# A fused attention and feed-forward kernel: a rebuilt opening, and pair sums of pattern tiles moved from VectorE to DMA transfers

## The chip, the cores and the metric

The kernel runs on one core of a Trainium2 chip. The core has five engines that run side by side, each through its own list of instructions in order: TensorE (PE in the profile) for matrix products, ScalarE (ACT) for functions such as the exponential, VectorE (DVE) for elementwise work, GpSimd (POOL), and SyncE (SP), which issues DMA transfers. They meet only through semaphores. The metric is the device time of one execution in microseconds (us); the median of several runs is given.

## The reference

The kernel computes a transformer layer in its parallel form: one normalised input feeds an attention with 32 query heads and one shared key and value head, and a feed-forward part with a squared ReLU. Both results are added to the input.

```python
S, D, H, Dh, F = 2048, 640, 32, 20, 1536
xn = layernorm(x)                                    # over the last axis, no scale or shift
q = (xn @ wq).reshape(1, S, H, Dh).transpose(0, 2, 1, 3)
k, v = xn @ wk, xn @ wv                              # one head of keys and values for all queries
p = softmax(einsum("bhqd,bkd->bhqk", q, k) * Dh ** -0.5)
o = einsum("bhqk,bkd->bhqd", p, v)
a = o.transpose(0, 2, 1, 3).reshape(1, S, H * Dh) @ wo
h = relu(xn @ w1 + b1) ** 2
out = x + a + h @ w2 + b2
```

## The kernel before, in words

**Blocks and tiles.** The queries are cut into 4 stretches of 512, the heads into 8 groups of 4. A stretch and a group make a block, and there are 32 blocks, worked off one after the other. Within a block the 2048 keys are 16 key tiles of 128. The scores of one key tile, one head and 512 queries are one tile of 128 x 512 in one of the eight banks of PSUM, so there are 32 x 16 x 4 = 2048 score tiles. Two to four of them are made at a time by matmuls that occupy different rows of TensorE's array (a score group). Everything else on TensorE runs as column groups: four matmuls side by side on 32 columns each.

**Two ways to an exponential.** ScalarE takes two or three neighbouring banks per instruction and writes the exponentials into slots of `PT` (`make_act`, L972; the instruction is L976). TensorE then multiplies them with the values (`make_pv`). The other way is a *set*: the four tiles of one key tile. VectorE makes from each tile of scores a line in the exponent of a bf16 number (`after_dqk`, instruction L1161, written as integers); three more copies, shifted by whole steps of the exponent's fraction, are made by GpSimd (L1181, an addition of 64-bit integers) or by VectorE (L1183). The weighted sum of the four copies stands for the exponential. So TensorE reads four pattern tiles for a set, two with the values `vx` and two with scaled values `vxs` (`make_dpv`). Where VectorE adds two of the copies beforehand (L1195, 128 x 2048 in one instruction, `dst = dst + src`), TensorE reads one column group less. A set that GpSimd and VectorE work on is kept in buffers of `tmore` and, once the input is no longer needed, of `x_sb`.

**The order.** The instruction lists are not written by hand. A planner in the kernel's own Python builds them: it keeps for each engine a queue of candidates with an assumed duration and assumed handover times (`Op`, `commit`, `LATS`), takes at each step the candidate that could start first, and orders ties by priorities (`prio`). `RULES` sets such priorities anew for each stage of 10 us of ScalarE's planned time, and `DEFAULTS` holds what no rule sets. Landings of DMA transfers are assumed too (`lat`), with a margin `DMARG` of 4 us. The plan decides the order on each engine and the semaphores that are waited for; on the chip each engine then goes through its list as fast as the waits let it. So the plan also decides how many tiles go to ScalarE and how many to sets.

**The opening.** The input's 16 row tiles (`x_sb`) are loaded, their mean and variance come from VectorE (L469 to L472) or, for the rows in `ACTST`, from ScalarE (L464, L465). Rows 0 to 3 get their reciprocal root by Newton steps on VectorE (L489 to L493), the others by a power on GpSimd (L481). L483 normalises a row, on VectorE or, for the rows in `POOLXN`, on GpSimd. TensorE transposes it with an identity matrix (L530 for rows 0 to 3, L594 for the others); the result is copied to `xnT`, by ScalarE (L532) or VectorE (L597). Keys follow (L546 for rows 0 to 3 one by one, `unit_KT` and L608 for four rows at a time), then queries and values. The identity is made by writing a staircase of zeros and one column of ones to DRAM (L428) and reading it back with a shifted stride (L435). Matmuls on constants (L525, L565) keep TensorE busy before.

**The other work.** The feed-forward part (L702, L710) and the output projections are cut into units that the planner puts between the score groups. A finished block is normalised by a chain of small transfers on SP's queue (`emit_norm`): sums to DRAM, back as a column (into `R`), their reciprocal on VectorE (L1048), to DRAM again, spread over the rows, and a product on VectorE (L1070). Eight transfers issued by GpSimd add the input to a tensor in DRAM on their way (L806).

The functions that the change touches:

Of the kernel before, what the change touches and what calls it, by code (L numbers as in the profile page):

```python
# [7 lines left out]
BF16 = mybir.dt.bfloat16  # L8
F32 = mybir.dt.float32
# [29 lines left out]
def _pl(z):  # L39
# [8 lines left out]
PTR = 20  # L48
# [3 lines left out]
STATIC = False  # L52
# [8 lines left out]
ADS = 1  # L61
# [5 lines left out]
NT = 9  # L67
# [7 lines left out]
DMEND = 1.0  # L75
SWITCH = 0.105
WARM = 0.72
WARM0 = 0.9

HOLD = dict(wq="TE2", b1="TE5", w1=("TE4", "TE6", "TE8", "TE10"), w2=("RL3_2", "RL3_4", "RL3_6", "RL3_8"), wo=("RL3_10", "FE24"), b2="VE8",  # L80
# [9 lines left out]
         2: {'KEEP': 1, 'JIT': 0.9},  # L90
         3: {'M1': 1},
         4: {'M1': 0, 'DRATE': 0.7, 'R3': 0, 'M1T': 0, 'PBIAS': 5},
         5: {'PVA': 1, 'SQP': 3, 'KEEP': 2},
         6: {},
         7: {'QKP': 0, 'D1P': 1, 'KEEP': 3},
         8: {'MPRIO': 0.9, 'ADP': 5, 'R3': -1},
         9: {'ADDN': 0.4, 'ND': 2},
         10: {'ADDN': 0.2, 'SQP': 0.7, 'M1T': 0, 'DRATE': 0.8, 'D1P': 1, 'URG': 3, 'JIT': 1.1, 'R3': 2},
         11: {'ADDB': 1, 'URG': 4, 'PP': 4, 'DRATE': 0.7, 'PVD': 0.9},
         12: {'ADDB': 1, 'BEHIND': 0.12, 'ADP': 0.9, 'DLAST': 2},  # L100
         13: {'EPS': 0},
         14: {'NOPEN': 1, 'EPS': 0.06, 'R3': 9, 'PP': 4},
         15: {'NOPEN': 1, 'EPS': 0.06, 'R3': 9, 'PP': 4, 'MRG': 0, 'DGAP': 0.8, 'ADP': 0.9},
         16: {'URG': 3, 'EVP': 0.3},
         17: {'ADDN': 0.2, 'M1T': 1.2},
         18: {'ADDN': 0.2, 'M1T': 1.2, 'MPRIO': 1.05},
         19: {'ADDN': 0.2, 'M1': 2, 'IDLE': 0.3, 'ND': 3, 'D1P': 0.5, 'ADP': 0.35, 'PVA': 1.05, 'QKP': 0},
         20: {'ADDN': 0.2, 'M1': 2, 'IDLE': 0.3, 'ND': 3, 'KEEP': 2, 'URG': 4, 'PP': 4, 'SQP': 3, 'ADP': 0.9},
         21: {'ADDN': 0.2, 'M1': 2, 'IDLE': 0.3, 'ND': 3, 'KEEP': 2, 'URG': 4, 'PP': 4, 'SQP': 3, 'ADP': 0.9, 'EPS': 0.12},
         22: {'PP': 2.5, 'NOPEN': 4},  # L110
         23: {'MPRIO': 0.3},
         24: {'PVD': 2.1, 'MPRIO': 1.05},
         25: {'DLAST': 2, 'EPS': 0, 'ADP': 0.35, 'ND': 3, 'R3': 1},
         26: {'NOPEN': 2, 'EVP': 0.3, 'EPS': 0.12},
         27: {'MRG': 0, 'URG': 2},
         28: {'ND': 1, 'ADP': 2, 'IDLE': 0.3},
         29: {'PBIAS': 0.6, 'M1': 2, 'ADDN': 0, 'SQP': 2},
         30: {},
         31: {'MRG': 0},
         32: {'NOPEN': 4, 'M1T': 0.6},  # L120
         33: {'NOPEN': 4, 'M1T': 0.6, 'MRG': 0, 'ADP': 3.5},
         34: {'R3': -1},
         35: {'ADDN': 0, 'DQP': 0.5, 'EPS': 0.12, 'MPRIO': 0.3},
         36: {'ADDN': 0, 'DQP': 0.5, 'EPS': 0.12, 'MPRIO': 0.3, 'NOPEN': 1},
         37: {'EVP': 1.1, 'ND': 2, 'M1T': 0.6},
         38: {'EVP': 1.1, 'ND': 2, 'M1T': 0.6, 'PBIAS': -1, 'PP': 0.9, 'PVA': 0.9},
         39: {'D1P': 1, 'ADP': 2},
         40: {'D1P': 1, 'ADP': 2, 'NOPEN': 2},
         41: {'D1P': 1, 'ADP': 2, 'NOPEN': 2, 'QKP': 0, 'JIT': 0.9},
         42: {'URG': 2, 'NOPEN': 2},  # L130
         43: {'URG': 2, 'NOPEN': 2, 'D1P': 1, 'DRATE': 0.7},
         44: {'PP': 2.5, 'R3': 1, 'NOPEN': 1, 'ADDN': 0},
         45: {'IDLE': 0.3, 'URG': 4, 'EVP': 0.8},
         46: {'IDLE': 0.3, 'URG': 4, 'EVP': 0.8, 'SQP': 3, 'ADDN': 0.6},
         47: {'IDLE': 0.3, 'URG': 4, 'EVP': 0.8, 'SQP': 3, 'ADDN': 0.6, 'DRATE': 0.8, 'DQP': 3},
         48: {'QKP': 0, 'M1T': 0.9, 'ADDN': 0.2, 'R3': 1},
         49: {'KEEP': 0, 'MPRIO': 0.5, 'DRATE': 0.7, 'R3': 0, 'NOPEN': 2},
         50: {'MRG': 0, 'URG': 2},
         51: {'MRG': 0, 'URG': 2, 'PVD': 1, 'DLAST': 6, 'M1T': 0},
         52: {'D1P': 3, 'R3': -1, 'DQP': 3},  # L140
         53: {'D1P': 1, 'KEEP': 1, 'PVD': 1, 'ADDN': 0, 'NOPEN': 1, 'DGAP': 1.5},
         54: {'D1P': 1, 'KEEP': 1, 'PVD': 1, 'ADDN': 0.2, 'NOPEN': 1, 'DGAP': 1.5, 'PBIAS': 5},
         55: {'D1P': 1, 'KEEP': 1, 'PVD': 1, 'ADDN': 0.2, 'NOPEN': 1, 'DGAP': 1.5, 'PBIAS': 1.5},
         56: {'D1P': 1, 'KEEP': 1, 'PVD': 1, 'ADDN': 0.2, 'NOPEN': 1, 'DGAP': 1.5, 'PBIAS': 1.5, 'URG': 3, 'ADP': 2},
         57: {},
         58: {'PVD': 0.9, 'DLAST': 3.5},
         59: {'ADDN': 0, 'EVP': 1.1, 'MRG': 0, 'DLAST': 3.5},
         60: {'ADDN': 0, 'EVP': 1.1, 'MRG': 0, 'DLAST': 3.5, 'M1T': 0, 'DGAP': 0},
         61: {},
         62: {'DGAP': 0.5, 'ADDN': 0.2, 'M1T': 0, 'JIT': 0.6, 'MRG': 9},  # L150
         63: {'DGAP': 0.5, 'ADDN': 0.2, 'M1T': 0, 'KEEP': 1, 'EVP': 0.8, 'IDLE': 0.3},
         64: {'PP': 0.9, 'NOPEN': 1, 'JIT': 0.9},
         65: {'DQP': 3, 'ADDN': 0, 'ADP': 2, 'NOPEN': 2},
         66: {'DQP': 3, 'ADDN': 0, 'ADP': 2, 'NOPEN': 2, 'ADDB': 1},
         67: {'ND': 1, 'R3': 1, 'PVA': 1, 'ADP': 2, 'D1P': 0.5},
         68: {'R3': -1, 'URG': 4}}
HOOK = None
PRIO = {}
NBEF = {}
# [14 lines left out]
QCPOS = 0  # L174
ACTST = (2, 5, 6)
POOLXN = (7, 9, 10, 11, 13, 14, 15)
# [8 lines left out]
DEFAULTS = dict(EVP=EVP, PBIAS=PBIAS, MPRIO=MPRIO, DGAP=DGAP, DLAST=DLAST, DRATE=DRATE, BEHIND=BEHIND, IDLE=IDLE, URG=URG, NOPEN=NOPEN,  # L185
                EPS=0.03, MRG=MRG, M1=M1, M1T=M1T, ADDN=ADDN, ADDB=0, ADP=3.5, JIT=JIT, R3=R3, STATIC=STATIC, PVA=1.05, PVD=1.05, D1P=0.5, PP=2.5, SQP=2, DQP=3, QKP=0, ND=2, WARM=WARM, KEEP=KEEP)

# [36 lines left out]
class Op:  # L224
    def __init__(self, name, eng, dur, parts, deps=(), lat=None, lock=False, mode="C", prio=3, dma=None):
        self.name, self.eng, self.dur, self.parts = name, eng, dur, parts
        self.deps = [d for d in deps if d is not None]
        self.lat, self.lock, self.mode, self.prio = lat, lock, mode, prio
        self.dma = dma
        self.start = self.fin = None  # L230
        self.consumed = False
        self.tgt = None
        self.clock = None
        self.frees = None
        self.after = None
        self.nb = 0.0
        self.blk = None
        if dma is not None:
            dma.n += 16
            self.tgt = (dma, dma.n)  # L240

    def ready(self):
        t = self.nb
        for d in self.deps:
            if d.fin is None:
                return None
            t = max(t, d.fin + (d.lat if d.lat is not None else LATS.get((d.eng, self.eng), 0.1)))
# [3 lines left out]
def bass_parallel_sum__grouped_kv_mqa__dense_activation_squared_relu__prompt_kernel(nc, A_x, A_wq, A_wk, A_wv, A_wo, B_x, B_w1, B_b1, B_w2, B_b2, out):  # L251
    es = ExitStack()
    with es:  # L253
# [59 lines left out]
        idd = nc.dram_tensor("idd", [128 * 128], BF16, kind="Internal").ap()  # L313
# [6 lines left out]
        eng_ctr = {k: newctr("m_" + k.lower()) for k in ENG if k != "SP"}  # L320
        osem = [newctr(f"osem{i}") for i in range(NOS)]
# [11 lines left out]
        lock_free = [0.0]  # L333
        pe_mode = ["C"]
# [9 lines left out]
        def commit(op):  # L344
# [4 lines left out]
            op.start, op.fin = s, s + op.dur  # L349
            free[op.eng] = op.fin  # L350
# [47 lines left out]
        def load(name, eng, fn, land, deps=()):  # L398
            return op(name, eng, 0.5, fn, deps, lat=land - 0.5, dma=one())
# [10 lines left out]
        stair = PT[:, PTR - 1, 0:128]  # L410
        z_ = op("idz", "DVE", 0.1, lambda e: e.memset(stair, 0.0), prio=-6)
        o_ = op("ido", "DVE", 0.08, lambda e: e.memset(stair[:, 0:1], 1.0), [z_], prio=-5)
# [6 lines left out]
        idw = []  # L419
# [8 lines left out]
        idw.append(load("IW", "SP", lambda e: e.dma_start(idd[0:128 * 128].rearrange("(p n) -> p n", p=128), stair), 2.2, [o_]))  # L428
# [5 lines left out]
        idd_rows = bass.AP(idd.tensor, 0, [[127, 128], [1, 128]])  # L434
        c_id = load("IR", "SP", lambda e: e.dma_start(ident[:], idd_rows), 2.2, idw)  # L435
        l_wq = load("wq", "SP", lambda e: e.dma_start(wq_sb[:, :, 80:D], wqv[:, :, 80:D]), 8.0, [HOLD["wq"]])
        w1v = B_w1.rearrange("(p dt) f -> p dt f", p=128)
        l_w1 = [load(f"w1{k}", "SP", lambda e, k=k: e.dma_start(w1_sb[:, :, 384 * k:384 * k + 384], w1v[:, :, 384 * k:384 * k + 384]), 8.0, [HOLD["w1"][k]]) for k in range(4)]
        l_b1 = load("b1", "SP", lambda e: e.dma_start(b1row[:], B_b1.rearrange("(f p) -> f p", p=128)), 8.0, [HOLD["b1"]])
        w2v = B_w2.rearrange("(ft p) d -> p ft d", p=128)  # L440
        l_w2 = [load(f"w2{k}", "SP", lambda e, k=k: e.dma_start(w2_sb[:, 3 * k:3 * k + 3, :], w2v[:, 3 * k:3 * k + 3, :]), 8.0, [HOLD["w2"][k]]) for k in range(4)]
        wov = A_wo.rearrange("(c p) n -> p c n", p=128)
        l_wo = [load(f"wo{c0}", "SP", lambda e, c0=c0, c1=c1: e.dma_start(wo_c[:, c0:c1, :], wov[:, c0:c1, :]), 8.0, [HOLD["wo"][k]]) for k, (c0, c1) in enumerate(((0, 3), (3, NCH)))]
# [14 lines left out]
        def rows(st):  # L458

            p = ROWP[st // 4]  # L460
# [1122 lines left out]
```

## Time and profile before

| | |
|---|---|
| median of 3 runs | 702.53 us (702.27 to 707.2) |
| profiled execution, from the first to the last instruction | 695.6 us |
| median less that span | 6.9 us |
| TensorE busy | 678.3 us, 98% |
| ScalarE busy | 673.4 us, 97% |
| VectorE busy | 606.7 us, 87% |
| GpSimd busy | 471.5 us, 68% |
| mean granted TensorE clock | 0.993, and 0.77 in the first 22 us |
| first and last exponential of ScalarE | starts at 22.05 us, ends at 686.7 us |

The profiled execution is one execution; its span leaves out what lies before the first and after the last instruction, and its own device time is taken as span and 6.9 us, which is the median. Matmuls are pipelined and the profile models their ends, so TensorE's 98% is the share of time with some matmul under way and not a share of its peak. The rows of the profile give for a group of instructions the line of the kernel, the engine, the operation, what is written and read, the shapes and the count; behind the bar the time in which at least one of them ran, the mean duration of one in nanoseconds, and the engine's idle time just before them with what ended it.

### The profile page before, as it was taken

Reading aid. Unit: us, or ns where it says so; the run is one execution under the profiler, and the core shown is the slowest. Engines: PE = TensorE matmul, PEld = TensorE weight load, DVE = VectorE, ACT = ScalarE, POOL = GpSimd, SP = SyncE. Lnnn points to the kernel's source line nnn. Section 1 sums busy time; section 2 is a strip of 40 time slices with the busy share of each in tenths; the row PEclk is TensorE's granted clock in tenths of the full one; section 3 lists DMA queues with packets and bytes.
Section 4 is the critical chain, followed back from the end, with each engine's and each line's share of the span. In section 5 each row is a group of like instructions: output and inputs, shape, how many; then the busy total and the mean of one; then the engine's idle time right before and its main releaser. Section 6 shows DMA issues by size and latency. Waiting matters only on the chain.

```text
span 695.6 us, 22438 instructions
## 1 busy us (share of the span) xinstructions
PE 678.3 (98%) x9683; PEld 214.6 (31%) x9685; DVE 606.7 (87%) x1028; ACT 673.4 (97%) x731; POOL 471.5 (68%) x474
## 2 busy tenths in 40 slices
PE   5899999999999999999999999999999999999997
PEld 3432223233222233332322233332322233333223
DVE  5859899998899998899789988889899998998984
ACT  4899999999999999999999999999999999999994
POOL 0526758788768877667558575787746756786873
PEclk7999999999999999999999999999999999999999
DMA  5414722257342221210200111011200211111101
GB/s 170 125 41 125 181 79 79 89 139 177 85 99 47 51 67 42 57 50 23 53 24 16 34 32 56 23 51 33 55 24 21 99 38 41 50 39 32 32 12 40
DMA packets 42304, 44.07 MB, mean 63 GB/s; under 512 B 15828, under 2 KB 33060, under 8 KB 42076
## 3 DMA queue, kind: packets, MB, share of 16 engines
q1 hardware_dynamic: 39420, 37.00, 19.2%
q0 software_dynamic: 2208, 5.25, 3.8%
q8 instruction: 76, 1.25, 0.7%
q10 hardware_dynamic: 576, 0.38, 0.2%
q14 instruction: 24, 0.20, 0.1%
HBM read 28.06 MB, written 14.94 MB: 62 GB/s over the span
## 4 chain that ended last, share of the span: by engine, by line
ACT 92%; PE 5%; DMA 1%; SPq 0%; DVE 0%; issue 0%; DVEq 0%
ACT PT L976 92%; PE ps L402 4%; DMA ident<-idd 1%; PE ps L594 1%; PE ps L530 0%; SPq L422 0%; DVE out_sb L1256 0%; PE ps L622 0%; PE ps L565 0%; PE ps L551 0%; SPq L430 0%; DVE PT L1256 0%; DVEq L253 0%; SPq L428 0%; DVE hT_tmp L408 0%
## 5 line engine op out<-in xcount | busy, mean ns | idle before, releaser
L976 ACT ACTIVATE PT<-ps 128x1024 bf16<-128x1024 f32 (+1 forms) x709 | 663.3, 1216 | 2.4 <-PE ps L402 2.4
L1161 DVE TENSOR_SCALAR tmore<-ps 128x512 uint16<-128x512 f32 x600 | 390.9, 685 | 49.0 <-PE ps L402 43.2
L1181 POOL INT64_ADD x_sb<-tmore x245 | 252.2, 1045 | 70.8 <-DVE tmore L1195 21.7
L1181 POOL INT64_ADD tmore<-tmore x196 | 201.3, 1041 | 115.7 <-DVE big L710 39.9
L402 PE MATMUL ps<-qT,kT 20*128 20x512 bf16 x2048 | 269.9, 384 | 2.6 <-ACT PT L976 1.6
L402 PEld LDWEIGHTS ps<-qT,kT 20*128 20x128 bf16 x2048 | 68.4, 91 | 271.6 <-ACT PT L976 240.1
L402 PE MATMUL ps<-PT,vx 128*32 128x512 bf16 x1448 | 134.6, 386 | 1.4 <-ACT PT L976 1.4
L402 PE MATMUL ps<-w_sb,big 128*32 128x320 bf16 x1536 | 75.6, 302 | 0.2 <-DVE tmore L1161 0.2
L402 PE MATMUL ps<-xnT,w_sb 128*32 128x512 bf16 x960 | 75.5, 383 | 0.0
L402 PE MATMUL ps<-tmore,vx 128*32 128x512 bf16 x796 | 73.3, 383 | 0.0
L402 PE MATMUL ps<-x_sb,vxs 128*32 128x512 bf16 x792 | 71.9, 382 | 0.0
L402 PEld LDWEIGHTS ps<-PT,vx 128*32 128x32 bf16 x1448 | 34.2, 94 | 58.5 <-issue 50.3
L1195 DVE TENSOR_TENSOR tmore<-tmore 128x2048 bf16<-128x2048 bf16 x37 | 47.0, 1273 | 0.0
L702 DVE TENSOR_SCALAR hT_tmp<-ps,b1col 128x512 bf16<-128x512 f32 x48 | 35.8, 746 | 8.1 <-PE ps L402 7.8
L402 PEld LDWEIGHTS ps<-w_sb,big 128*32 128x32 bf16 x1536 | 32.8, 95 | 29.8 <-issue 22.0
L402 PE MATMUL ps<-tmore,vxs 128*32 128x512 bf16 x396 | 35.7, 382 | 0.0
L402 PE MATMUL ps<-xnT,wq_sb 128*32 128x512 bf16 (+1 forms) x480 | 33.6, 364 | 0.0
L402 PE MATMUL ps<-wo_c,OC 128*32 128x320 bf16 x608 | 31.2, 302 | 0.0
L402 PEld LDWEIGHTS ps<-xnT,w_sb 128*32 128x32 bf16 x960 | 18.6, 95 | 25.3 <-issue 20.2
L402 PEld LDWEIGHTS ps<-tmore,vx 128*32 128x32 bf16 x796 | 19.3, 95 | 20.0 <-issue 13.4
L402 PEld LDWEIGHTS ps<-x_sb,vxs 128*32 128x32 bf16 x792 | 19.0, 95 | 16.0 <-issue 10.9
L1044 DVE COPY OR<-ps 128x512 f32<-128x512 f32 x30 | 20.6, 685 | 2.3 <-PE ps L402 1.9
(89 smaller groups left out, 287.6 us busy)
## 6 DMA issues: line engine op xcount, KB each, us to landing
xbd<-b2d SPq DMA_DIRECT2D x16, 320.0 KB, 4.4
xbd<-in_A_x_dram POOLq DMA_DIRECT2D x8, 640.0 KB, 5.8
xr<-xbd SPq DMA_DIRECT2D x32, 160.0 KB, 2.4
w_sb<-in_B_w_dram SPq DMA_DIRECT2D x8, 480.0 KB, 4.2
big<-OR SPq DMA_DIRECT2D x71, 40.0 KB
big<-drs SPq DMA_DIRECT2D x71, 40.0 KB
out_dram<-out_sb SPq DMA_DIRECT2D x15, 160.0 KB, 1.9
qT<-QCr SPq DMA_DIRECT2D x108, 20.0 KB
```

The source lines that it names most:

```text
L402: return lambda e: e.matmul(out_, l, r, start=start, stop=stop, tile_position=tp)
L594: return [(lambda e, dt=dt: e.transpose(out=psbf(bk)[:, dt * 128:(dt + 1) * 128], in_=xn_sb[:, st, dt:D:DT], identity=ident[:])) for dt in ...
L702: o = Op(f"RL{qc}_{f}", "DVE", 0.66, [lambda e: e.tensor_scalar(out=hT_tmp[:, k % 2, :], in0=ps[:, bk, :], scalar1=b1col[:, f:f + 1], scal ...
L976: return Op(f"ACT{st_['j']}", "ACT", 0.05 + 0.4267 * n, [lambda e: e.activation(out=PT[:, s0:s0 + n, :], in_=ps[:, b0:b0 + (n - 1) * db + ...
L1044: tn = op(f"TN{b}", "DVE", 0.60, lambda e: e.tensor_copy(out=OR[:, a, :], in_=ps[:, PVB, :]), [lastpv] + or_users[a], prio=0)
L1161: d1 = op(f"D1_{n}_{i}", "DVE", 0.60, lambda e: e.tensor_scalar(out=L[:, cs].bitcast(U16), in0=ps[:, bank, :], scalar1=XA, scalar2=XB, op0 ...
L1181: fn = lambda e, T=T, j=j: e.int64_add(out=T.bitcast(I64), in0=L.bitcast(I64), in1=TSTEP * j * 0x0001000100010001)
L1195: p = op(f"AD{a}_{n}" if q == ADS - 1 else f"AE{a}_{n}_{q}", "DVE", 0.065 + 1.066 / ADS, lambda e, src=src[:, w], dst=dst[:, w]: e.tensor_ ...
```

## The change

**The opening.** The identity is computed on VectorE: five instructions build a ramp 0, 1, ..., 31 by doubling, a transpose within blocks of 32 turns it to a column, and four comparisons write the diagonal blocks. The two transfers are gone. The copies of rows 1 and 3 to `xnT` go from ScalarE to VectorE. ScalarE sums rows 2 and 4 instead of 2, 5 and 6. GpSimd normalises row 8 and no longer row 13. Keys of rows 4 to 15 are made for two rows at a time, in six units instead of three. Before the first product with values, idle time of TensorE is always filled with matmuls on constants. The first two units of later queries come behind the last rows instead of in the middle.

**The pair sums.** In 114 places the sum of two pattern copies is an accumulating transfer issued by GpSimd, from one buffer into the other, each with one of eight semaphores in turn; 6 sums remain on VectorE, where 54 stood. The planner assumes for these transfers a time on GpSimd (`ADDUR`), a start (`ADLEAD`), an occupation of the DMA engines (`ADGAP`, together with other wide transfers) and a landing (`ADLAND`).

**The rest.** The landing of the column of sums gets 5 us more of margin (`SLX`). `PT` has 16 slots instead of 20, the pattern copies have one buffer more (`NT`). All rules by stage and the defaults are new, and the planner may add more tiles to a score group (`P2`, `MRG`, `M1`). By the built programs, ScalarE's exponentials are 701 instructions of two tiles, 4 of three and 2 of one, where there were 667, 36 and 6; sets cover 632 tiles instead of 600; the shifted copies are 434 on GpSimd (441 before) and 40 on VectorE (9 before).

```diff
-PTR = 20
+PTR = 16
...
-NT = 9
+NT = 10
...
+SLX = 5.0
+NADS = 8
+ADDUR = 0.92
+ADPL = 0.1
+ADLEAD = 2.3
+ADLAND = 3.6
+ADGAP = 3.1
...
-ACTST = (2, 5, 6)
-POOLXN = (7, 9, 10, 11, 13, 14, 15)
+QCPOS = 2
+ACTST = (2, 4)
+SPLITK = (1, 2, 3)
+FIRSTP = {"T": 0.3, "K": 0.25, "Q": 0.9}
+TEDVE = (1, 3)
+POOLXN = (7, 8, 9, 10, 11, 14, 15)
...
             op.start, op.fin = s, s + op.dur
+            if op.add:
+                begun = max(s + ADLEAD, dma_free[0])
+                dma_free[0] = begun + ADGAP
+                op.lat = begun + ADLAND - op.fin
+            elif op.dw > 0:
+                dma_free[0] = max(dma_free[0], s + 1.5) + op.dw
...
-        stair = PT[:, PTR - 1, 0:128]
-        z_ = op("idz", "DVE", 0.1, lambda e: e.memset(stair, 0.0), prio=-6)
-        o_ = op("ido", "DVE", 0.08, lambda e: e.memset(stair[:, 0:1], 1.0), [z_], prio=-5)
+        ramp, ramp_t = (PT[:, PTR - 2 + k, 0:64].bitcast(F32) for k in range(2))
+        r_ = op("idr", "DVE", 0.08, lambda e: e.memset(ramp[:, 0:1], 0.0), prio=-6.5)
+        z_ = op("idz", "DVE", 0.1, lambda e: e.memset(ident[:], 0.0), prio=-6)
+        for k in (1, 2, 4, 8, 16):
+            r_ = op(f"id{k}", "DVE", 0.145, lambda e, k=k: e.tensor_scalar(out=ramp[:, k:2 * k], in0=ramp[:, 0:k], scalar1=float(k), scalar2=None, op0=ALU.add), [r_], prio=-5)
+        t_ = op("idt", "DVE", 0.2, lambda e: e.transpose(out=ramp_t, in_=ramp), [r_], prio=-5)
+        c_id = [op(f"ide{k}", "DVE", 0.1, lambda e, w=slice(32 * k, 32 * k + 32): e.tensor_scalar(out=ident[w, w], in0=ramp[w, :], scalar1=ramp_t[w, 0:1], scalar2=None, op0=ALU.is_equal),
+                   [z_, t_], prio=-5) for k in range(4)]
...
-        idw.append(load("IW", "SP", lambda e: e.dma_start(idd[0:128 * 128].rearrange("(p n) -> p n", p=128), stair), 2.2, [o_]))
...
-        idd_rows = bass.AP(idd.tensor, 0, [[127, 128], [1, 128]])
-        c_id = load("IR", "SP", lambda e: e.dma_start(ident[:], idd_rows), 2.2, idw)
...
+            if st in TEDVE:
+                te = op(f"TE{st}", "DVE", 0.40, lambda e, st=st, cs=cs: e.tensor_copy(out=xnT[:, :, cs], in_=psbf(st)[:, 0:DT * 128].rearrange("p (dt n) -> p dt n", dt=DT)), [t_], prio=-1)
+            else:
...
                 misc.append(unit_T(st))
-            misc.append(unit_KT(c))
+                if c in SPLITK and st % 2 == 1:
+                    misc.append(unit_KT(st // 2, 1))
...
-            d2 = op(f"SL{b}", "SP", 0.5, lambda e: e.dma_start(R4[:, a, :], drs[b, 0].rearrange("(p n) -> p n", p=128)), [d1, r4_user.get(a)], lat=1.6 + marg, dma=nr4[a])
+            d2 = op(f"SL{b}", "SP", 0.5, lambda e: e.dma_start(R4[:, a, :], drs[b, 0].rearrange("(p n) -> p n", p=128)), [d1, r4_user.get(a)], lat=1.6 + marg + SLX * (marg == DMARG), dma=nr4[a])
...
+                    if s["add"][a] == "DMA":
+                        k = nadd[0] % NADS
+                        nadd[0] += 1
+                        p = op(f"AD{a}_{n}", "POOL", ADDUR, lambda e, src=src, dst=dst: e.dma_start(dst, src, accum_op=ALU.add), dp + [ad_last.get(k)], dma=adsem[k], prio=par("ADPM"))
...
-                while pick[0] > free["PE"] + (0.1 if pe_mode[0] == "C" else 0.3) and pe_share(free["PE"] + 0.2) < (par("WARM") if pv_begun else WARM0):
+                while pick[0] > free["PE"] + (0.1 if pe_mode[0] == "C" else 0.3) and (not pv_begun or pe_share(free["PE"] + 0.2) < par("WARM")):
```

## The prediction

> **What bounds the kernel now.** I read the chain that ended last first: whatever is on it sets the time.
>
> ```profile
> by line: ACT PT L976 92.4%; PE ps L402 3.7%; DMA ident<-idd 1.0%; PE ps L594 0.5%; PE ps L530 0.3%; SPq L422 0.3%; issue 0.3%; DVE out_sb L1256 0.2%; PE ps L622 0.2%; PE ps L565 0.1%; PE ps L551 0.1%; SPq L430 0.1%; DVEq L253 0.1%; DVE PT L
> ...
> 5.12 7.27 DMA ident<-idd
> 12.39 0.14 issue
> 12.53 2.30 PE ps L530 x20
> ...
> 41.82 638.56 ACT PT L976 x682
> ```
>
> ScalarE's exponential (L976) is 92% of the chain, unbroken from 41.8 us to 680.4. Before it stands an opening whose longest piece is one transfer, the identity's way through DRAM, 7.27 us. Next the groups by shape, ScalarE and the pattern work on VectorE:
>
> ```profile
> L976 ACT ACTIVATE PT<-ps 128x1024 bf16<-128x1024 f32 x667 | 620.8, 1200 | 1.1 <-PE ps L402 1.1
> L976 ACT ACTIVATE PT<-ps 128x1536 bf16<-128x1536 f32 x36 | 57.3, 1601 | 1.4 <-PE ps L402 1.4
> L976 ACT ACTIVATE PT<-ps 128x512 bf16<-128x512 f32 x6 | 3.7, 619 | 0.0
> ...
> L1161 DVE TENSOR_SCALAR tmore<-ps 128x512 uint16<-128x512 f32 x600 | 390.9, 685 | 49.0 <-PE ps L402 43.2
> L1195 DVE TENSOR_TENSOR tmore<-tmore 128x2048 bf16<-128x2048 bf16 x37 | 47.0, 1273 | 0.0
> L1195 DVE TENSOR_TENSOR x_sb<-x_sb,tmore 128x2048 bf16<-128x2048 bf16 x15 | 19.4, 1293 | 0.0
> ```
>
> The idle time before L976 is 2.5 us in all: ScalarE is the bound. Its tiles are 667x2 + 36x3 + 6 = 1448 of the 2048; the other 600 go by patterns through L1161. The instructions overlap, so the means (1200) overstate: from the records' starts, a 1024-wide one follows the last by 917 ns on average (median 904) and a 1536-wide one by 1341. TensorE is close behind. In the timeline 0.32 us lie between a score group and the column group that follows it, 0.32 back, 0.22 between column groups of 512 and 0.136 of 320. So a score group costs 0.22 + 2 x 0.105 (two changes) = 0.43. 683 score groups x 0.43, 1272 column groups of 512 x 0.216 and 552 of 320 x 0.136 are about 641 us, 96% of the 664.7 us for which ScalarE runs (22.05 to 686.7). Last the transfers:
>
> ```profile
> q1 hardware_dynamic: 39420, 37.00, 19.2%
> q0 software_dynamic: 2208, 5.25, 3.8%
> ...
> xbd<-in_A_x_dram POOLq DMA_DIRECT2D x8, 640.0 KB, 5.8
> ```
>
> The 16 engines are 24% busy. The last line is the only accumulating transfer of the trace.
>
> **The change, part by part.** *ScalarE's tiles.* By the order of the built program L976 becomes 701 of 1024, 4 of 1536 and 2 of 512: 1416 tiles, 32 fewer. At the cadences above: 34 x 0.917 = +31.2; 32 x 1.341 = -42.9; 4 of 512 fewer at about 0.75 = -3.0. **-14.7 us**, on the path.
>
> *Who takes them.* VectorE gets 32 more L1161 (390.9/600 = 0.65 each: +20.8) and 31 more shifted passes (18 at 0.85, 13 at 0.69: +24), and loses 48 of 54 sums (69.2/54 = 1.28: -61.5); with +3.5 in the opening -13, so 607 becomes 594, 88% of a span of 674. POOL loses 7 passes (453.5/441 = 1.03: -7) and issues 114 transfers (0.885 by L806: +101): 471 becomes 565, 84%. TensorE loses 8 column groups of PT and 34 of patterns (a summed pair is read once) and gains 7 fills: -35 x 0.216 = -7.6, about 633 us for ScalarE's 650, 97%. The score groups are 684. Nobody is over the bound, but TensorE's spare falls from 23.7 to 16.2 us.
>
> *The transfers.* Each reads 0.52 MB, reads 0.52 MB of destination and writes it. The row above (0.33 MB in; 0.66 MB read and written) took 3.8% of 695.6 us over 8 = 3.3 us of the 16 engines. By bytes written that makes 2.6 us, by all three streams 3.2, by elements added 5.3. I take 3.2, as it counts what moves. 114 x 3.2 = 365 us, and the engines rise from 24% to some 79%. A landing took 5.4 to 6.5 us from the issue when alone (six transfers), 5.8 and 7.0 when two overlapped. In the built order 12.9 us of TensorE's cadence (median) lie between a set's last score group and the first read of a summed pair; in one in ten under 10.5. Needed are 0.2 + 0.69 (L1161) + 0.17 + one to three passes of 1.04 + 5.7: 7.8 to 9.9. So the median has 3 us to spare and the tight tenth under 1. Behind a late one TensorE's whole queue waits, then ScalarE. Two of the six lone landings were 0.7 us over the rest; a third of 114 late by 0.7, a quarter of these uncovered, is some 7 us, of which ScalarE's lead of a step hides about half: **+3 us**; below it 0, above it the rival of late landings. [...]
>
> *The opening.* The first exponential starts at 22.05. The identity becomes 12 small VectorE instructions (at 0.2, the cadence of L491-L493, some 1.8 us) where VectorE waited 1.90 us for rows: nothing, or 0.3 if they overhang. SP issues two transfers fewer (0.44, 0.60), so the rows behind them come earlier. The statistics of rows 0-3 and the Newton steps are as before: the first normalised row starts at 9.43. Then transposes 10.3 to 11.6 (37 warm-up matmuls: 7 at 0.4, the others at 0.215 from 4.1 us, end near 10.3); copies to xnT alternate between ScalarE (0.71) and VectorE (0.49) instead of 4 on ScalarE: last at 12.3. Keys, then four queries at 0.39 per block of 20 (its price at full clock at 18.00; the blocks from 15.2 to 17 paid 0.5 under a mean granted clock of 0.77 up to 22 us): 13.6; copy 0.28 and three handovers of 0.2: scores at 14.6, exponential at 15.0 to 15.6. **-6.5 us**; bounds -2.3 (the identity alone, if the other queues keep the pace) and -7.5. Next late are the keys: ScalarE eats two rows' keys in 4 x 0.917 = 3.7 us. VectorE needs 4.2 for two rows (each 1.0 of statistics by the cadence of L469 to L472, 0.36 to normalise by L483, 0.41 to copy by L597, 0.3 for the keys), less the seven rows that POOL normalises and the one that ScalarE sums, and it starts on them near 12.3, 11 us before the first pair is due; keys for two rows at a time instead of four come half as coarse. I leave ScalarE's 2.4 us of early gaps as they are.
>
> *At nothing.* The reciprocal's longer margin (SLX) only moves L1048 later in VectorE's order; it shows no idle time now. 16 slots for PT instead of 20: a slot's reader has 8 x 0.917 = 7.3 us instead of 9.2; TensorE's being abreast hides it, and without it ScalarE waits (in the rival of TensorE). The tail from 686.7 to 695.6 stays.
>
> Sum: -14.7 - 6.5 + 3 = -18.2. The profiled span is 695.6; around it I put 6.9, which makes the median of 702.5 (lowest 702.3, highest 707.2). **684.3 us, say 684.**
>
> **The rivals.** *Keys starve the early start* (10%): VectorE's opening work, 12.6 us up to 22 and 17.2 of the next 20, is as long as before, and one more row's statistics is on it. Then the 6.5 us go: 691. Against: it stood idle 3.77 us before L544, waiting for the identity's late keys.
>
> *TensorE is the bound* (12%): if its 23.7 us of waiting are handovers that remain, ScalarE's stretch is 633 + 24 = 657 instead of 650, and with the opening and the 3 us: 692. For: weight loads waited 245.6 us for L976, so both stand in lockstep; against: that is TensorE waiting for ScalarE.
>
> *Late landings* (13%), slower: each transfer delays TensorE by a mean d, and ScalarE has no queue to live on. Break-even at 21.2/114 = 0.19 us. At 0.3, +34: 715; the stretch is 698 to 735. For: the tight tenth above, engines three times as busy, and one of L806's eight issues held POOL 1.08 us where others took 0.83 to 0.88. [...]
>
> *The transfers saturate* (6%), slower: at 5.3 us each they need 604 us, and with 167 of others 771 of busy engines, so some 776. It decides from (672 - 167)/114 = 4.4 us.
>
> **How the numbers follow.** The forecast of 684 holds 59% (677 to 691); the rivals 10, 12, 13 and 6. The range of 675 to 707 leaves out the transfers' saturation, most of the late landings and the lower edge. A measurement here tells 1% (7 us). Faster by over 1%, under 695.5: the forecast and the first two rivals less their tails, 0.73; within 1%, 0.11: these tails and mild lateness; slower 0.16: the rest.
>
> **What would show it.** The first L976 (L994 after) near 15.3; 707 of them at 0.92 with under 5 us of idle before them; the new transfers' queue at about 52% and landings near 5.7; the sums' row on VectorE nearly gone. Wrong if idle time shows on ScalarE behind TensorE, and on TensorE behind DMAs into tmore or x_sb; if ScalarE has gaps between 20 and 45 us, the keys were it.

## The result and the profile after

The changed kernel takes **706.2 us** (median of 20 runs, 699.9 to 720.1) where the kernel before takes 701.8 in the same session. The ratio is **1.0056, 95% interval 1.003 to 1.0082**: slightly slower, where 684 was forecast. The executions of one kernel differ with TensorE's mean granted clock (the changed kernel took 699.9 us at 0.988 and 720.1 at 0.960), so medians are loose, and the ratios leave the longest executions out: a ratio can lie below 1 where the median of all lies above.

The profiled execution has a span of 704.8 us, 9.2 more than before. The pair is not alike, though. In all executions whose span and time are both on record, the time is 1.8 to 2.0 us over the span. So the 6.9 us that were put around the span of 695.6 do not belong there: this execution of the kernel before took some 697.5 us, at the short end of that kernel's times (mostly 696 to 703), and between the medians the change costs 4.4 us. What follows is the account of the profiled pair.

I split ScalarE's stretch by the starts of its exponentials: what lies between two starts beyond the usual distance (904 ns after a tile pair, 1331 after three, 490 after one) is called *excess* here.

| us | before | after | forecast of the difference | measured |
|---|---|---|---|---|
| first exponential starts | 22.05 | 15.58 | -6.5 | -6.5 |
| 709 and 707 exponentials at their usual distance | 653.8 | 640.0 | -14.7 | -13.8 |
| excess between them | 10.9 | 39.8 | +3 | **+28.9** |
| from the last one's end to the end | 8.9 | 9.4 | 0 | +0.5 |

So both gains came, and a third term ate them. The groups of the changed kernel by shape, and two rows of VectorE:

```profile
L994 ACT ACTIVATE PT<-ps 128x1024 bf16<-128x1024 f32 x701 | 646.7, 1166 | 28.6 <-PE ps L416 28.6
L994 ACT ACTIVATE PT<-ps 128x1536 bf16<-128x1536 f32 x4 | 5.9, 1484 | 0.0
...
L994 ACT ACTIVATE PT<-ps 128x512 bf16<-128x512 f32 x2 | 1.5, 758 | 0.0
...
L1183 DVE TENSOR_SCALAR tmore<-ps 128x512 uint16<-128x512 f32 x632 | 410.5, 684 | 66.0 <-PE ps L416 59.2
...
L1066 DVE RECIPROCAL R<-R 128x16 f32<-128x16 f32 x30 | 7.3, 244 | 11.2 <-DMA R<-drs 11.2
```

ScalarE now sits idle 28.6 us for TensorE, 2.5 before. The last row is the surprise: the reciprocal of a block's sums holds VectorE 11.2 us, in two waits, for an 8 KB transfer. Before, it had no idle time:

```profile
L1048 DVE RECIPROCAL R<-R 128x16 f32<-128x16 f32 x30 | 7.3, 243 | 0.0
```

The transfers after:

```profile
q0 software_dynamic: 18624, 65.02, 49.3%
q1 hardware_dynamic: 39132, 36.93, 19.0%
...
x_sb<-tmore POOLq DMA_DIRECT2D x57, 512.0 KB, 5.5
tmore<-tmore POOLq DMA_DIRECT2D x54, 512.0 KB, 5.6
...
xbd<-in_A_x_dram POOLq DMA_DIRECT2D x8, 640.0 KB, 10.2
```

The new transfers' queue holds 49.3% of the engines' time (52 forecast) and a pair sum lands after 5.5 to 5.6 us (5.7). The wide accumulating transfer of the input needs 10.2 us where it needed 5.8. TensorE's own waits:

```profile
PE ps L416 <- DVE tmore L1183: 9.9, 4, 8.6
PE ps L416 <- DVE OR L1062: 3.3, 1, 3.3
...
PE ps L416 <- DMA tmore<-tmore: 0.9, 2, 0.5
```

It hardly waits for a pair sum (0.9 us in all, and its weight loads 1.7); it waits for VectorE, once 8.6 us and once 3.3. In the excess by place there are three long waits, with what follows them: near 46 us (6.7 us), near 78 (10.1, and 3.9 more until 100) and near 193 (3.4, and some 3 more). The chain of waits around the second:

```profile
66.38 19.17 DMA R<-drs
85.55 0.03 issue
85.57 0.25 DVE R L1066
85.82 0.56 DVE tmore L1183
86.38 0.05 issue
86.42 11.88 PE ps L416 x75
```

The column of sums of block 0 is issued at 66.38 and lands 19.17 us later (7.58 in the kernel before). VectorE's list stands still at the reciprocal, and behind it wait the pattern copies that free TensorE's banks. What TensorE does around it (columns: window and length; busy time with counts for TensorE, its weight loads, VectorE, ScalarE, GpSimd; granted clock; share of the 16 DMA engines; GB/s):

```profile
core 0: us, PE busy (x) PEld busy (x) DVE busy (x) ACT busy (x) POOL busy (x), PEclk, DMA share, GB/s
42.00:66.00 24.00, 23.92 (x355) 8.22 (x351) 20.30 (x38) 17.04 (x19) 7.92 (x8) 1.00 0.21 53
78.00:88.00 10.00, 1.57 (x13) 0.48 (x13) 2.42 (x5) 1.18 (x2) 0.44 (x1) 0.66 0.83 207
88.00:98.00 10.00, 10.00 (x77) 1.86 (x72) 4.23 (x8) 6.03 (x6) 3.91 (x4) 0.50 0.74 181
```

Near 46 us (first row) it is ScalarE alone that stands, 17 of 24 us busy; TensorE works without a break on 26 column groups of FFN1 that its list holds ahead of block 1's first scores. From 78 to 88 all five columns are nearly empty. Then comes a loss that no term of the sum held: during the 8.64 us of idleness TensorE's clock falls to 0.50, and it stays there until 98, some 12 us after TensorE goes on. A column group takes 0.40 to 0.43 us instead of 0.22, and 6 exponentials fall into the window (13 in the mended order below).

Why is an 8 KB transfer late? The transfers issued between 55 and 95 us, before and then after (KB each, median us to landing):

```profile
w_sb<-in_B_w_dram SPq DMA_DIRECT2D x4, 480.0 KB, 5.6
xbd<-b2d SPq DMA_DIRECT2D x4, 320.0 KB, 5.4
...
R<-drs SPq DMA_DIRECT2D x2, 8.0 KB, 5.5
```

```profile
w_sb<-in_B_w_dram SPq DMA_DIRECT2D x4, 480.0 KB, 14.8
xbd<-b2d SPq DMA_DIRECT2D x4, 320.0 KB, 6.9
...
R<-drs SPq DMA_DIRECT2D x1, 8.0 KB, 19.2
```

The same four loads of w2 and four broadcasts of a bias run in both. But the loads of w2 were issued at 60.1, 70.9, 82.9 and 88.7 us before, and at 61.8, 63.0, 64.7 and 72.7 after: each waits for a unit of FFN1 that frees its place, and those units now run in a row. Three of the loads stand ahead of the column of sums on SP's queue, where one stood before, and two pair sums and two accumulating transfers of the input are issued between 63 and 76 us. The column lands 0.75 us behind the last of the three loads; before, it landed 0.15 us behind the last wide transfer ahead of it. Hence two theories: the *place in the queue*, and the *traffic* of the accumulating transfers.

### The profile page after: what moved, and what is told of

Same layout as the page of the kernel before. It is cut to its first block, busy times and chain, and to the rows that moved or that the text cites. A ratio compares the mean times of both kernels' runs of the same rounds, so it can differ in the third digit from the quotient of the medians.

```text
span 704.8 us, 22498 instructions
## 1 busy us (share of the span) xinstructions
PE 683.4 (97%) x9624; PEld 214.9 (30%) x9624; DVE 592.2 (84%) x1061; ACT 659.4 (94%) x723; POOL 565.8 (80%) x581
## 3 DMA queue, kind: packets, MB, share of 16 engines
q0 software_dynamic: 18624, 65.02, 49.3%
## 4 chain that ended last, share of the span: by engine, by line
ACT 54%; PE 27%; DMA 8%; DVE 6%; POOL 2%; issue 1%; SPq 0%; DVEq 0%; POOLq 0%
ACT PT L994 54%; PE ps L416 26%; DMA R<-drs 4%; DMA tmore<-tmore 3%; DVE tmore L1183 3%; DMA cmore<-drs 2%; PE ps L583 1%; POOL tmore L1203 1%; DVE hT_tmp L722 1%; POOL x_sb L1203 1%; DMA drs<-R 1%; DVE big L730 0%; DVE x_sb L1205 0%; DVE OR L1062 0%; DVE QCr L686 0%
## 5 line engine op out<-in xcount | busy, mean ns | idle before, releaser
L994 ACT ACTIVATE PT<-ps 128x1024 bf16<-128x1024 f32 (+1 forms) x707 | 652.0, 1167 | 28.6 <-PE ps L416 28.6
L1183 DVE TENSOR_SCALAR tmore<-ps 128x512 uint16<-128x512 f32 x632 | 410.5, 684 | 66.0 <-PE ps L416 59.2
L1203 POOL INT64_ADD tmore<-tmore x222 | 251.5, 1261 | 40.4 <-DVE tmore L1183 19.4
L1203 POOL INT64_ADD x_sb<-tmore x212 | 242.3, 1269 | 46.9 <-DVE tmore L1183 21.6
L1218 POOL DMA_DIRECT2D tmore<-tmore x54 | 59.4, 1100 | 4.9 <-POOL tmore L1203 2.2
L1218 POOL DMA_DIRECT2D x_sb<-tmore x57 | 60.4, 1069 | 2.7 <-POOL x_sb L1203 2.7
L416 PE MATMUL ps<-tmore,vxs 128*32 128x512 bf16 x608 | 57.5, 392 | 0.3 <-POOL tmore L1203 0.3
L416 PE MATMUL ps<-x_sb,vxs 128*32 128x512 bf16 x612 | 56.8, 387 | 0.1
L416 PE MATMUL ps<-tmore,vx 128*32 128x512 bf16 x512 | 48.6, 386 | 0.9 <-DMA tmore<-tmore 0.9
L416 PE MATMUL ps<-x_sb,vx 128*32 128x512 bf16 x316 | 31.2, 385 | 0.0
## 6 DMA issues: line engine op xcount, KB each, us to landing
xbd<-in_A_x_dram POOLq DMA_DIRECT2D x8, 640.0 KB, 10.2
```

The costliest lines, as they stand in the source:

```text
L416: return lambda e: e.matmul(out_, l, r, start=start, stop=stop, tile_position=tp)
L994: return Op(f"ACT{st_['j']}", "ACT", 0.05 + 0.4267 * n, [lambda e: e.activation(out=PT[:, s0:s0 + n, :], in_=ps[:, b0:b0 + (n - 1) * db + ...
L1183: d1 = op(f"D1_{n}_{i}", "DVE", 0.60, lambda e: e.tensor_scalar(out=L[:, cs].bitcast(U16), in0=ps[:, bank, :], scalar1=XA, scalar2=XB, op0 ...
L1203: fn = lambda e, T=T, j=j: e.int64_add(out=T.bitcast(I64), in0=L.bitcast(I64), in1=TSTEP * j * 0x0001000100010001)
L1218: p = op(f"AD{a}_{n}", "POOL", ADDUR, lambda e, src=src, dst=dst: e.dma_start(dst, src, accum_op=ALU.add), dp + [ad_last.get(k)], dma=adse ...
```

## The experiments

All edits but the small sums are made on the finished plan: instructions change places within an engine's list. Beyond that, e6 and e8 add matmuls on constants, and e11 and e12 have those of e8; e12 and e13 let four passes wait for another product. Names are the planner's: `w20` to `w23` load w2, `XC` broadcast the bias, `XB` add the input on their way, `SL` and `RS` bring a block's sums in and their reciprocals out, `QD` move queries.

**e0_after_again**, the unchanged kernel.

> The changed kernel once more, as the reference of this group. Both theories: 706 us, and the same three long waits of ScalarE (near 46, 78 and 193 us) if they belong to the order of the instructions; if they are chance landings of single transfers, those at 78 and 193 move or vanish from one execution to the next.

Measured 708.1 us, 1.0066 (1.0015 to 1.0118). The three waits came back at 46.0 (6.70 us), 78.1 (10.8) and 194.1 (4.6), the column of sums landing after 19.6 us: they belong to the order, not to chance.

**e1_small_sums**

```diff
-e.dma_start(dst, src, accum_op=ALU.add)
+e.dma_start(dst[:, 0:64], src[:, 0:64], accum_op=ALU.add)
```

> Every pair-sum transfer moves 64 of 2048 columns; order, issues and waits stay, so most of the sums are left out and the output is not the reference's. Theory 'traffic' (the accumulating transfers slow the small transfers of SP's queue): the column of sums lands within 8 us, the waits near 78 and 193 go with what follows them, 14 and 6 us: 684 to 688. Theory 'place in the queue' (the column stands behind two loads of w2 that were not ahead of it before, with or without traffic): the wait near 78 stays for the most part: 698 to 702. Rival 'late sums hold TensorE directly': only the 2.4 us that TensorE waited for transfers into tmore go: 703 to 704.

692.7 us, 0.9873 (0.9805 to 0.994): between the two theories. The column still stands behind the loads of w2 and lands after 13.2 us; the reciprocal waits 3.6 us instead of 10.0. So traffic is part of it and the queue alone keeps 13 of the 19 us. The wait near 193 is gone, but in this profile the clock is at 0.50 from 19 to 49 us and all that follows lies some 11 us later, so whether the traffic or the shift took that wait away is not separated here.

**e2_w2_behind**

```diff
 XC14 w20 XC15
-w21 w22
 SL0
+w21 w22
 QD4_3 QD5_0 ...
```

> Two loads of w2 are issued behind the column of sums of block 0 instead of ahead of it; nothing else moves. 'Place in the queue': the column lands in 8 to 10 us instead of 19.2, the reciprocal waits under 1 us, the stall near 78 and its aftermath go: 10 to 14 us less, 692 to 696. 'Traffic' alone: the column still lands after 15 us or more and the time stays within 3 us of 706.

The profiled span is 690.8 us, the median 700.5, ratio 0.9953 (0.9904 to 1.0003). The column lands after 11.8 us and the reciprocal waits 1.6 us: the queue's part is right. But the gain is not steady, because something else is late next, as its chain of waits and TensorE's waits between 74 and 95 us show:

```profile
72.72 0.64 DVE tmore L1183
73.36 15.82 DMA w_sb<-in_B_w_dram
89.18 0.14 issue
```

```profile
PE ps L416 <- DMA w_sb<-in_B_w_dram: 4.6, 1, 4.6
```

The last load of w2, issued behind seven transfers of queries, lands 15.8 us later, and TensorE waits for it. Taking one transfer out of a jam leaves the jam.

**e3_w2_cm**

```diff
 (VectorE) SQ0_0
-CM0_1
 CM0_2 TN6 RL0_1 D1_33_0 RC5 D1_32_3 D1_33_1 RL0_2 SQ0_1 SQ0_2 D1_33_2
+CM0_1
```

> As the run before, and the product of block 6's chain (L1088, the one that waited 3.6 us at 190 us for rows from DRAM) stands nine instructions later in VectorE's list. If VectorE's standing still in its list is what turns a late small transfer into idle time of ScalarE: a further 3 to 7 us, 686 to 692. If the wait only moves to the next user of the rows: as the run before.

702.0 us, 1.0007 (0.9965 to 1.0049): no different from e2 by these numbers. It tells nothing on its question, since I had taken the wrong product: the one that waits reads `cmore`, and that is `CM0_2`. (By the built lists the product moved past eleven instructions; the expectation says nine.) What its profile, of an execution of 711.8 us, gives is how long a fall of the clock can last: TensorE stands still for 2.0 us at 85.9, and the clock is granted at 0.50 from 89 to 130 us, with TensorE busy all that time.

**e4_spread**

```diff
 (SP) XC12 XC13
-XC14
 w20
-XC15 w21 w22
 SL0
+w21 w22 w23
 QD4_3 QD5_0 ... QD6_1
-w23
 RS0
-wo0
+XC14 XC15
 ...
 (wo0 behind wo3, XR28 and XR29 behind FW27; on GpSimd XB14 behind P3_6)
```

> Only the order on two queues is changed: on SP three loads of w2 stand behind the column of sums, two broadcasts of the bias, a load of wo and two reads of the input's sum stand later; on GpSimd one of the accumulating transfers of the input comes seven instructions later. Theory 'jam' (between 60 and 88 us the 16 engines are full, and whatever small transfer lies in it turns late): the jam is spread, the column lands within 9 us, none of reciprocal, w2 and column is waited for over 1 us, and ScalarE's waits over the cadence fall from 40 us to 17 to 22: 685 to 690. Rival 'another small transfer takes the place': a wait of 4 us or more stays between 75 and 95 us, 692 to 700.

**687.4 us, 0.9812 (0.9778 to 0.9846)**, four executions within 686.4 to 688.6: it beats both kernels. By the built lists XB14 moves past ten instructions; the expectation says seven. The column lands after 6.8 us, the waits near 78 and 193 are gone, the excess is 21.4 us; the longest wait of a reciprocal is 1.6 us, at 651. ScalarE's row and the same windows as above:

```profile
L994 ACT ACTIVATE PT<-ps 128x1024 bf16<-128x1024 f32 (+1 forms) x707 | 651.0, 1168 | 11.2 <-PE ps L416 11.0
```

```profile
42.00:66.00 24.00, 23.92 (x370) 8.52 (x362) 19.92 (x37) 17.04 (x20) 7.45 (x8) 1.00 0.20 48
78.00:88.00 10.00, 10.00 (x145) 3.34 (x145) 7.19 (x13) 10.00 (x12) 6.99 (x8) 1.00 0.91 220
88.00:98.00 10.00, 10.00 (x161) 3.26 (x153) 8.27 (x15) 10.00 (x13) 7.93 (x9) 1.00 0.99 238
```

The DMA engines are fuller than in the changed kernel (0.91, 0.99). They may be: the column of sums now stands behind one load of w2 and lands 0.2 us after it. Same work, same plan, same bytes: 18.4 us of excess were a matter of the order on two queues.

**e7_small_spread**, the order of e4 with the small sums of e1.

> The order of the spread run with pair-sum transfers of 64 of 2048 columns (most of the sums left out). If the sums' traffic costs only through the jam near 75 us: the same time as the spread run within 2 us. If it goes on costing elsewhere (late landings that hold TensorE, slower small transfers in every block): 4 us or more below the spread run, 680 to 684.

685.3 us, 0.9783 (0.9746 to 0.9821), a span of 682.9. With the order mended the pair sums' traffic costs 2.1 us (687.4 less 685.3), so it is not free elsewhere but nearly so. In the order as planned it costs 1.9%, some 13 us, by the ratios (1.0066 in e0, 0.9873 in e1). The rival of the prediction in which late pair sums hold TensorE is thereby bounded at some 2 us. The column's landing divides in the same way. Behind one load of w2 it takes 6.8 us with the traffic (e4) and 6.8 without (e7); behind three it takes 13.2 without (e1) and 19.2 with it. So the two further loads, with the two broadcasts that e4 also moved away, are worth 6.4 us of its delay, and the traffic adds 6.0 only behind them.

**e6_fill**: the changed kernel, and on TensorE

```diff
 QK59
+fill x38
 DQK6_0
```

> The changed kernel with 38 column groups of zeros (0.22 us each, 8.4 us) on TensorE ahead of the group that waits near 78 us for the reciprocal to let VectorE go on; they add nothing to the result. Theory 'standing still halves the clock' (TensorE idle from 77.8 to 86.4, then each group at 0.41 to 0.45 us instead of 0.22 until 97): the long wait stays at 9 to 11 us, but the granted clock stays over 0.9 behind it and the 4 to 5 us of short waits after it go: 700 to 702. Rival 'the clock falls for another reason at that place': 0.5 to 0.6 between 85 and 95 us as before, 705 to 708.

The windows of this run:

```profile
78.00:88.00 10.00, 9.31 (x164) 4.06 (x156) 2.70 (x6) 0.76 (x2) 0.00 (x0) 1.00 0.83 206
88.00:98.00 10.00, 10.00 (x153) 3.21 (x145) 6.74 (x12) 10.00 (x12) 7.87 (x8) 1.00 0.75 187
```

The wait for the reciprocal stays (9.5 us), the clock stays at 1.00, and the excess from 75 to 100 us falls from 14.0 to 9.6 us, all of it the wait itself. So here it is TensorE's standing still that halves the clock, by one profile of each kernel (from 88 to 98 us 0.50 in the changed kernel, 1.00 here). The time is not as clear: 705.5 us, 1.0046 (1.001 to 1.0083), against 1.0056 for the changed kernel; the wait near 190 us remained in this run, with the clock at 0.71 behind it. The 4 us are shown in the trace and not in the median.

**e5_spread_hoist**: the order of e4, and on TensorE

```diff
 FFN3_0.0 FFN3_0.1 PV0_15 FFN3_0.2
+QK32 QK33
 FFN3_0.3 ... FFN3_2.1
+QK34
 FFN3_2.2 ... FFN3_3.0
+QK35 PV1_0
 ...
```

> As the run before, and block 1's first score groups and products with values come up to 5.6 us ahead of the 26 column groups of FFN1 that stood before them (the pattern groups follow the next score group). Theory 'handed-back opening' (ScalarE stands 6.7 us near 46 for scores that could be made at once): 4 to 6 us less than the run before. Theory 'TensorE owes this work' (from the 30th to the 160th step TensorE's list holds 8.3 to 9.1 us for each ten steps of ScalarE's 9.0 to 9.2, so there is room for 2 to 3 us only): the one long wait becomes some twenty short ones, and the time is 0 to 2 us less than the run before, or more by the lost pairing of groups.

709.2 us (median of ten, 695.0 to 722.8), 0.996 (0.9917 to 1.0003), a span of 701.2: much worse than e4. The one wait of 6.7 us became seventeen of up to 2.3 us, 20 us in all between 44 and 92, and TensorE, fed in pieces, had its clock at 0.5 to 0.86 from 60 to 90. In the executions with the clock at 1.00 it takes 695 to 697, still 8 more than e4. The edit also broke up pairs of score groups, so a smaller one was made.

**e9_hoist_small**: the order of e4, the same groups 1.1 us earlier, pairs kept.

> The spread run with the first score groups of block 1, pattern groups with them, 1.1 us ahead in TensorE's list; the lead is gone after 8 us of other work. Pairs of groups stay together, which the larger hoist broke up. 'ScalarE stands for nothing': the wait near 46 us falls to 5.6 and the time by 1 us. 'TensorE owes the work': the wait is made up behind it, 687 as the spread run.

702.7 us, 0.9922 (0.9881 to 0.9962); in its one execution with the clock at 1.00, 690.3 where e10 has 687.0 and 687.3. The wait did fall to 5.84 us, and more than that was lost between 50 and 75 us (excess 8.3 instead of 0.2), in a profile of 705.4 us whose clock was at 0.51 from 57 to 67. Neither hoist gains anything. That fits a TensorE that owes these 26 column groups. Whether a new plan could spread them over the next hundred steps stays open; no list was found by hand in which banks and pairs allow it.

**e8_late_open**: the order of e4, and on TensorE 30 more warm-up matmuls ahead of the first transpose.

```diff
+fill x30
 T0
```

> The spread run with 30 more warm-up matmuls on TensorE ahead of the first transpose (6.5 us). It asks whether the earlier opening is worth its 6.5 us at the end, or is given back at the wait near 46 us. 'Given back': the wait shrinks by what the start is later, and the time is 687 to 689. 'Kept': the wait stays at 6 to 7 us, only later, and the time is 692.5 to 694.

The 30 matmuls cost 8.5 us and not 6.5: the first exponential starts at 23.7 us instead of 15.2 (e10, of the same group), and the wait of block 1 is 6.70 us as ever, now at 53.4: nothing is given back. A later start is a later end, in full: of the 12.8 us by which the span of 698.1 exceeds e10's, 8.5 are the start and 4.1 excess. The run lost more (706.7 us, 1.0028 (0.9979 to 1.0076)) because, shifted so, the third long wait reappears at 187 us, which e4 does not show.

**e11_late_cm** was to tell whose wait that is, with the product of e3.

> The late-opening run with the product of L1088 that waited 3.0 us near 187 us for rows from DRAM put nine instructions later in VectorE's list. 'VectorE's list turns a late small transfer into idle time': the wait of 3.0 us, the 2.8 us of ScalarE and the fall of the clock behind it go, ScalarE's waits between 175 and 200 us fall from 6 us to under 1.5, and the profiled span is 692 to 694 instead of 698. 'The rows are late for whoever comes': GpSimd's pass that waited 5.1 us for this product waits longer, and as much is lost within 15 us of it.

704.1 us, 1.0054 (1.0026 to 1.0082), and the waits stayed (2.3 us on TensorE, 3.4 on the product). The waiting product stood where it had stood: here the mistake of e3 was found.

**e12_late_cm2** moves the right one, and four GpSimd passes that were kept behind it follow the product ahead of it instead:

```diff
 (VectorE) SQ0_0 CM0_1
-CM0_2
 TN6 RL0_1 D1_33_0 RC5 D1_32_3 D1_33_1 RL0_2 SQ0_1
+CM0_2
```

> The late-opening run with the product of L1088 that reads cmore (the third of its stage; the run before had moved the second, which does not wait) six instructions later in VectorE's list, and the four GpSimd passes that were kept behind it put behind the product ahead of it. 'VectorE's list turns a late small transfer into idle time': the wait of 3.0 us on VectorE, the 2.8 us on ScalarE and the halved clock behind them go, ScalarE's waits from 175 to 200 us fall from 6 us to under 1.5; 692 to 696 for the profiled span. 'Late rows hold whoever comes': the waits stay over 4 us and only move.

698.1 us, 0.9959 (0.9927 to 0.999), a span of 695.8. The waits between 180 and 200 us in the late opening, VectorE's and what TensorE waited for behind it:

```profile
DVE OC L1088 <- DMA cmore<-drs: 3.0, 1, 3.0
...
PE ps L416 <- DVE OR L1062: 2.7, 1, 2.7
```

With the product moved (past eight instructions; the expectation says six) neither row is left; the clock stays at 1.00 there and the excess from 175 to 200 us falls from 6.0 to 1.2. So the third wait too is VectorE's list: a product whose first user, those four passes apart, is planned 40 us later stood in order ahead of `TN6`, the copy that frees TensorE's bank. In the changed kernel the same product waits 3.6 us for its rows, and TensorE 3.3 behind it.

**e13_spread_cm2**: e4 with this move; **e10_spread_again**: e4 on another occasion.

> The spread run with the same move. Its own executions show no wait near 180 us, so the time stays at 686 to 688; if the moved product or the passes cost anything, over 689. If the executions of the spread run at 690 us and over had this wait, they go.

> The spread run once more, on another occasion: 687 us, 1.5 to 2.2% under the kernel before, and no wait between 60 and 100 us.

687.8 us, 0.9819 (0.9787 to 0.9852), and 689.2, 0.9832 (0.9794 to 0.987): both are e4 within their intervals. The move neither costs nor gains where the wait is not seen. e4 holds up: **1.7 to 1.9% faster than the kernel before**.

## Why the prediction was wrong, step by step

*The tiles of ScalarE*, -14.7: right, -13.8. *The opening*, -6.5: right, and to the tenth by luck: the first exponential starts at 15.58 where 15.0 to 15.6 was given, and between 14.7 and 16.1 in the other runs with this opening. By e8 it counts in full. *The transfers*: 49.3% of the engines' time for 52, landings of 5.5 for 5.7, GpSimd 565.8 us busy for 565, VectorE 592 for 594. With the order mended the sum of these terms is 695.6 - 13.8 - 6.2 + 0.5 + 10.5 of more excess = 686.6; e4's span is 686.7. So the two gains came as they were reasoned.

The sizes need care. The span that the sum gave was 695.6 - 18.2 = 677.4, and e4's is 9.3 more, mostly by the excess. That its 687.4 us lie near 684 is luck: 6.9 us were put around the span where 1.8 to 2.0 belong. That 706.2 lies between 675 and 707 is luck as well, since the upper part of that range was held for TensorE as the bound and for mildly late pair sums, and what came were two late small transfers. And in spans e4 gains 8.9 us, 1.3%. The 1.9% are of medians and hold some 5 us more, by which most executions of the kernel before are longer than its profiled one (701 to 703 us at a mean clock of 0.985, some 697 at 0.993). No trace shows where they lose it.

Four places failed, all in the term for waits, +3 against +28.9.

**"At nothing. The reciprocal's longer margin (SLX) only moves L1048 later in VectorE's order; it shows no idle time now."** This is the step that failed first. It followed VectorE's list and not the queue on which the column of sums arrives. The trace of before already held a hint: the median landing of these columns was 2.2 us, but 7.6 for block 0, issued 1.2 us behind a load of w2. The built order showed two more such loads ahead of it. Measured: 19.2 us, a wait of 10.0.

**The "+3 us"** was an allowance for late pair sums that hold TensorE. They held its matmuls for 0.9 us and its weight loads for 1.7, and with the order mended they cost 2.1 us in all (e7), so this size was near. The rival of late landings (13%, 715) was right that landings would turn late and wrong about whose: it priced 114 equal delays with a break-even of 0.19 us each, and two small transfers made some 20 us between them. By e1 and e4 it takes both the sums' traffic and the order: either one mended removes most of it.

**"[T]he engines rise from 24% to some 79%"** is a mean. It came out at 69%, and either number says nothing of a stretch. The rival of saturation asked for 4.4 us a transfer over the whole span, which was not in sight; but from 66 to 78 us the engines were full (a share of 1.02) and to 88 at 0.83, with loads of w2, bias and input in one heap.

**"Next late are the keys."** The keys were never late. Next late was block 1's first score group behind 26 column groups of FFN1 in TensorE's list, 6.7 us, in every run that leaves this stretch of the list as planned. It stood in the built order and was overlooked. It is no loss of the opening (e8), and e5 and e9 say that moving it alone gains nothing. That the same row of FFN1 units bunched the loads of w2 is argued from their order and issue times; no run shows it by itself.

And one term was missing: what follows a wait. A stall was taken to cost its length; behind each of the two long ones of TensorE came 3 to 4 us from the halved clock (0.50 until 98 us, and from 197 to 204).

The other rivals: the keys left no gap over 1 us between 20 and 45 us. TensorE as the bound (12%) can't be told from the rest to a microsecond: in e4 ScalarE's stretch is 661.4 us where the forecast had 650 and this rival 657, but 6.7 of its 21.4 us of excess are the one wait at 46.

The mark "wrong if idle time shows on ScalarE behind TensorE" was met; "and on TensorE behind DMAs into tmore or x_sb" was not: TensorE stood behind VectorE.

## What to carry to other kernels

When a change fills the DMA engines, list the small transfers that an in-order engine waits for, and for each what is issued ahead of it on its queue and in its own few microseconds; a share over the whole span hides the stretch that decides (here 69% over the span, and 1.02 from 66 to 78 us). An instruction whose result is not needed soon, but which waits for a transfer, belongs behind the copies that free another engine's buffers (in e12 that took the excess around it from 6.0 to 1.2 us). Before a plan is given up, its lists are worth reordering by hand: here the same plan went from 0.6% slower to 1.7 to 1.9% faster.

## What the runs showed of the hardware

**The clock fell after short waits, and for long.** In these profiles every gap of TensorE of 1.7 us and more was followed, within 4 us of its start, by a granted clock of 0.50: gaps of 2.0 us in e3 (at 85.9), 2.5 in e6 (188.4), 2.7 in e8 (187.3), 8.6 in the changed kernel. Of the gaps of 0.7 to 1.4 us some were (1.3 us in e3, at 671.0) and most were not (1.3 us in e4, at 652.2). The clock came back 4 to 17 us after the end of such a gap (4 after the 4.6 us of e2, 12 after the 8.6), and in e3 42 us after the 2.0. With equal lists, the unchanged kernel took 700.7 us at a mean granted clock of 0.987 and 710.5 at 0.976 within one group of runs.

**An accumulating transfer's price in a full system.** A pair sum of 512 KB lands after 5.5 to 5.6 us, one of 16 KB (e7) after 2.6 to 2.7: an estimate of 5.7 us per MB, some 175 GB/s, from these two, though the 16 engines are 69% busy beside the first and 30% beside the second.

**A queue's small transfers waited for its large ones.** In e1, without the sums' bytes, 8 KB behind three loads of 480 KB landed after 13.2 us, 0.4 us behind the last of them. In 14 of the 16 profiles block 0's column lands 0.15 to 1.0 us behind the last wide transfer ahead of it on SP's queue, in e2 and e3 2.3 and 3.6 us. The median landing of these columns is 2.2 us before, 4.0 after, and 2.2 in e7.

**GpSimd's passes stretched in the records only.** The 64-bit additions last 1.17 us (median) beside the transfers, where 1.04 was the length before, but follow each other at 1.014 us as ever; with the small sums of e7 they are as long (1.19), so it is not the bytes. An issue of a pair sum holds GpSimd 1.07 to 1.10 us where the issue of the accumulating transfers before took 0.89.
